# Batch 0's transposed tokens in banks by head pairs; batch 2's first M quarter ahead of one piece of output and its scores behind another

## The chip, the core and the metric

The kernel runs on one core of a Trainium2 chip. The metric is device time in microseconds (us) of one execution; the kernel before has a median of 202.16 us over three runs (202.1 to 202.26). TensorE is written PE in the profile's rows (its weight loads PEld), VectorE DVE, ScalarE ACT, GpSimd POOL and SyncE SP. SP, ACT and POOL also issue DMA transfers; a q behind an engine's name (SPq, POOLq) marks what its queue does. Each engine works through its own list of instructions strictly in order, and waits at an instruction whose semaphores have not come.

## The reference, cut to what matters

There are 8 batches with 8 heads, 512 tokens and 32 state rows of 64 numbers for each head. Attention runs in both directions between tokens and state rows, the two results are laid side by side as rows of 512 numbers, and a two-layer network is applied to every row:

```python
def _attn_ref(x, state):
    scores = scale * np.matmul(x, state.transpose(0, 1, 3, 2))
    a = softmax(scores)                      # over the 32 state rows, 1e-9 in the divisor
    xread = np.matmul(a, state)
    scores2 = scale * np.matmul(state, x.transpose(0, 1, 3, 2))
    a2 = softmax(scores2)                    # over the 512 tokens
    sread = np.matmul(a2, x)
    return np.concatenate([xread, sread], axis=2)

def _moe_ref(x, w_in, w_out):
    h = x @ w_in                             # 512 -> 2048
    g = np.maximum(0.01 * h, h)
    return g @ w_out                         # 2048 -> 512
```

## The kernel before

**What is computed, and in which form.** For the token rows the kernel never forms `xread`. It multiplies the state by the first weight matrix once per batch, M = state · w_in (2 x 128 rows, 2048 columns), and then h = a · M. M is made in four quarters of 512 columns: `a_m(a, c, tag)` (L364) makes quarter c in PSUM banks of the tag given, and `m_evict` (L384) copies it to SBUF. `ff1(a, hT, j)` (L394) makes 128 columns of h as two products over the probabilities `a.aT` and M, in one bank of tag "ph", and ACT applies the leaky relu on the way to `hT` (L403). For batch 0 `piece(0, h0, i, jq)` (L602) multiplies one quarter jq of h by w_out for a quarter i of the tokens; four such pieces make one output bank, which `y_store` copies out (ACT or DVE) and SP stores. From batch 1 on, class `Batch` does the second layer with 7 products instead of 8 (Strassen), in units of two products (`f.unit`, L679), on two banks of tag "py".

**Banks.** Tags "ph" and "py" have two banks each and are handed round in turn; "big" and "sc" are one tile of two banks each. A new user of a bank waits until the last copy out of it has ended. Pieces (0, 0) and (0, 1) hold "py" banks, pieces (0, 2) and (0, 3) the two halves of "big"; batch 1's second layer takes the "py" banks over, bank 1 from piece (0, 0), bank 2 from piece (0, 1).

**The scores chain of a batch.** `a_scores` (L212) makes the scores in "sc" from the transposed tokens `a.xT` and the transposed state. On DVE `a_shift` follows (row maxima L226, spread L234, subtraction L239), `a_max2` (L288, L290), and after an exponential on ACT (L246) `a_probs` (sum L251, L255, reciprocal L258, spread L263, product L264) gives `a.aT`. `a_exp2` on ACT (L296) reads "sc" too and is its last reader. From batch 1 on, xT comes by a DMA transpose that SP issues (L200) once POOL and ACT have cast the batch's tokens; batches 2 and 3 take their state from `st_t[0]`, a DMA transpose issued by SP (L187) behind a cast on POOL (L186).

**The order of the work.** It is written out by hand: the program sets the order on each engine (`manual_schedule`), and nothing is moved by a planner. The parts that matter here:

- The head, 0 to about 10 us. Batch 0's tokens come as four transfers of two heads each (`xf`), and are cast to bf16 by DVE, ACT and POOL (L120). PE transposes them (`x0_half`, L781), for each half u of the tokens into two banks, one for each quarter of the tokens, all four head pairs k in each; `xt0_evict` (L789) copies each bank out, one on DVE and one on ACT. Scores (L796, L811) and maxima (L831) follow.
- POOL issues the loads of w_in (L126), of w_out (L134), of batch 1's tokens (L900) and of batch 2's (L107), in that order; the last load is the last quarter of w_out, which pieces of quarter jq = 3 need.
- From L1000 on PE runs batch 0's sixteen pieces of the second layer, and between them makes batch 1's scores and M and batch 2's first M quarter; from L1063 it adds batch 1's `ff1`.

Of the kernel before, what the change touches and what calls it, by code (L numbers as in the profile page):

```python
# [9 lines left out]
P = 128  # L10
# [6 lines left out]
NK = H // 2  # L17
# [5 lines left out]
BF16 = mybir.dt.bfloat16  # L23
# [7 lines left out]
def kernel(  # L31
# [9 lines left out]
    nc = tc.nc  # L41
# [9 lines left out]
    psum = ctx.enter_context(tc.tile_pool(name="psum", bufs=2, space=bass.MemoryType.PSUM))  # L51
# [5 lines left out]
    VEC, SCA, POO = nc.vector.tensor_copy, nc.scalar.copy, nc.gpsimd.tensor_copy  # L57
# [20 lines left out]
    ident = consts.tile([P, P], BF16, name="ident")  # L78
# [33 lines left out]
    def cast_x(b, h0, h1, copy):  # L112
        copy(  # L113
            xs[b][:, :, h0:h1].rearrange("p t h d -> p h t d"),
            xl[b][:, h0:h1].rearrange("p h (t d) -> p h t d", t=NT),
        )

    def cast_x0(k, t0, t1, copy):
        h = 2 * (k % 2)
        copy(  # L120
            xs[0][:, t0:t1, 2 * k:2 * k + 2].rearrange("p t h d -> p h t d"),
            xf[k // 2][:, h:h + 2, D * t0:D * t1].rearrange("p h (t d) -> p h t d", t=t1 - t0),
        )
# [61 lines left out]
    def state_t(i):  # L185
        POO(stb[i][:], stf[i][:])  # L186
        nc.sync.dma_start_transpose(st_t[i][:], stb[i][:].rearrange("p b q -> p (b q)"))  # L187
# [17 lines left out]
    def st_of(a, g, k):  # L205
        rows = slice(D * g, D * (g + 1))
        if a.b == 0:
            return stbd[rows, k, g ^ (k // 2), :]
        t = st1 if a.b == 1 else st_t[0][:, a.b - 2] if a.b < 4 else st_t[1][:, a.b - 4]
        return t[rows, NS * k:NS * (k + 1)]  # L210

    def a_scores(a):  # L212
        sc = psum.tile([P, 2, S], FP32, name="sc", tag="sc", bufs=1)
        for k in range(NK):
            for g in range(2):
                nc.tensor.matmul(  # L216
                    sc[NS * k:NS * (k + 1), g, :],
                    lhsT=st_of(a, g, k),
                    rhs=a.xT[D * g:D * (g + 1), :, k, :],
                    start=True, stop=True,  # L220
                )
        a.sc = sc
# [141 lines left out]
    def a_m(a, c, tag):  # L364
        if a.M is None:
            a.M = mpool.tile([P, 2, DFF], BF16, name="M", tag="M")
        if tag in ("ph", "py", "phpy"):
            pm = [psum.tile([P, DM], FP32, name="pm", tag=t) for t in (tag[:2], tag[-2:])]
            at = [t[:] for t in pm]
        else:  # L370
            pm = psum.tile([P, 2, DM], FP32, name="pm", tag=tag, bufs=1)
            at = [pm[:, g, :] for g in range(2)]
        for k in range(NK):
            for g in range(2):
                v, r = (k // 2, 2 * (k % 2) + (g ^ (k // 2))) if a.b == 0 else (g, k)
                nc.tensor.matmul(  # L376
                    at[v][NS * r:NS * (r + 1)],
                    lhsT=st_of(a, g, k),
                    rhs=w_in_bf[D * g:D * (g + 1), k, DM * c:DM * (c + 1)],
                    start=True, stop=True,  # L380
                )
        return pm

    def m_evict(a, c, pm, copy):  # L384
        cols = slice(DM * c, DM * (c + 1))
        if isinstance(pm, list):
            for g in range(2):
                copy(a.M[:, g, cols], pm[g][:])
        else:
            copy(a.M[:, :, cols], pm[:])  # L390
# [211 lines left out]
    def piece(b, hT, i, jq, bank=None, copy=SCA, part=range(4)):  # L602
        if jq == 0:
            y = ys[b, i] = Y()
            y.py = psum.tile([P, DM], FP32, name="py", tag="py")[:] if bank is None else bank
        y = ys[b, i]
        for j in (4 * jq + v for v in part):
            nc.tensor.matmul(  # L608
                y.py, lhsT=hT[:, j, P * i:P * (i + 1)], rhs=w_out_bf[:, j, :],
                start=(j == 0), stop=(j == 15),  # L610
            )
        if jq == 3 and copy is not None:
            y_store(b, i, copy)

    def y_store(b, i, copy):
        tag, bufs = (f"yo{i - 2}", 1) if (b, i) in ((0, 2), (0, 3)) else ("ysb", 3)
        ysb = ypool.tile([P, DM], FP32, name="ysb", tag=tag, bufs=bufs)
        copy(ysb[:], ys[b, i].py)
        if b == B:
            for bb in range(4):  # L620
                r0 = (4 * i + bb) * SROW + S
                nc.sync.dma_start(out[r0:r0 + NS, :], ysb[NS * bb:NS * (bb + 1), :])
        else:
            nc.sync.dma_start(rows_of(b)[i], ysb[:])
# [143 lines left out]
    a0, a1, a2 = att_of[:3]  # L768
# [5 lines left out]
    state01()  # L774
    spin(3, "py")

    def x0_half(u):
        pxt = [psum.tile([P, NK, P], BF16, name="pxth", tag=("ph", "py")[u]) for _ in range(2)]
        for k in range(NK):
            for v in range(2):  # L780
                nc.tensor.transpose(  # L781
                    pxt[v][:, k, :],
                    a0.xb[:, 2 * u + v, 2 * k:2 * k + 2, :].rearrange("p h d -> p (h d)"), ident[:],
                )
        return pxt

    def xt0_evict(u, pxt, copies):
        for v, copy in enumerate(copies):
            copy(a0.xT[:, 2 * u + v], pxt[v][:])  # L789

    sct = {}

    def scores0(u, v):
        sct[u, v] = psum.tile([P, NK, 2, NS], FP32, name="sct", tag=("big", "sc")[v], bufs=1)
        for k in range(NK):
            nc.tensor.matmul(  # L796
                sct[u, v][:, k].rearrange("p w n -> p (w n)"),
                lhsT=a0.xT[:, 2 * u + v, k, :],
                rhs=stbd[:, k].rearrange("p g n -> p (g n)"),
                start=True, stop=True,  # L800
            )
# [5 lines left out]
    def rows0(u):  # L807
        scn[u] = psum.tile([P, 2, HT], FP32, name="scn", tag="ph")
        for q in range(2):
            for c in range(NK):  # L810
                nc.tensor.matmul(  # L811
                    scn[u][NS * c:NS * (c + 1), q, :], lhsT=stbd[:, 2 * q + c // 2, c % 2, :],
                    rhs=a0.xT[:, 2 * u:2 * u + 2, 2 * q + c // 2, :], start=(q == 0), stop=False,
                )
# [13 lines left out]
    def max0(u, v):  # L828
        if v == 0:
            m0[u] = att.tile([P, NG], FP32, name="m0", tag="m0")  # L830
        nc.vector.tensor_reduce(  # L831
            out=m0[u][:, H * v:H * (v + 1)],
            in_=sct[u, v][:].rearrange("p k w n -> p (k w) n"), axis=AX.X, op=ALU.max, negate=True,
        )
# [27 lines left out]
    def recip0(u):  # L862
        q = att.tile([P, NG], BF16, name="q0", tag="q0")
        with nc.allow_low_precision(reason="one rounding, of the finished reciprocal"):
            nc.vector.reciprocal(q[:], r0[u][:])
        return q
# [12 lines left out]
    cast_x0(0, 0, NT, VEC)  # L879
    for k in (1, 2):  # L880
        cast_x0(k, 0, 2, VEC)
    cast_x0(3, 0, 2, SCA)
    for k in (1, 2):
        cast_x0(k, 2, NT, VEC)
    cast_x0(3, 2, NT, POO)
    pxt = [x0_half(u) for u in range(2)]
    xt0_evict(0, pxt[0], (VEC, SCA))
    xt0_evict(1, pxt[1], (SCA, VEC))
    x1 = [consts.tile([P, NK, 2 * P], FP32, name="x1", tag=f"x1{u}") for u in range(2)]
    a0.aT = att.tile([P, 2, S], BF16, name="aT", tag="aT")  # L890
    open_xb(1)
# [12 lines left out]
        load_w_out(c, 3 - c)  # L904
    load_x(2, nc.gpsimd)
    load_w_out(3)
    for u in range(2):
        rows0(u)
    for v in range(2):
        scores0(1, v)  # L910
        max0(1, v)
    spread0(scn[0], m, False)
    exp0(0)
    for u in range(2):
# [1 line left out]
    pm = a_m(a0, 0, "big")  # L916
# [3 lines left out]
    q = recip0(0)  # L920
# [7 lines left out]
    q = recip0(1)  # L928
    pm = a_m(a0, 1, "big")
# [3 lines left out]
    h0 = hpool.tile([P, 16, S], BF16, name="hT", tag="hT")  # L933
# [42 lines left out]
    for u, j, tag in (  # L976
# [7 lines left out]
        if (u, j) == (0, 8):  # L984
            pm = a_m(a0, 3, "big")
# [15 lines left out]
    for u in range(2):  # L1001
        piece(0, h0, 1 + u, 0, bank=wide[:, 0] if u else None)
        ps = psum.tile([P, NT, 2, P], BF16, name="pxt2", tag="ph")
        for t in range(NT):
            for v in range(2):
                h = NK * u + 2 * v
# [16 lines left out]
    weights_sum(2, 0, 4, nc.gpsimd)  # L1023
    weights_sum(1, 0, 4, nc.gpsimd)
    state_t(0)
    cast_x(2, 0, 4, SCA)
    for h in range(NK, H):
        cast_x(2, h, h + 1, POO)
    a_open(a2, 2)
    a_xt_dma(a2)  # L1030
    for i in (2, 3):
        piece(0, h0, i, 1)
    m_evict(a1, 3, a_m(a1, 3, "ph"), SCA)
    for g in range(2):
        a_exp2(a1, g)
    load_x(3, nc.sync)
# [1 line left out]
    a_probs(a1)  # L1038
    for i in range(NT):
        piece(0, h0, i, 2)  # L1040
    piece(0, h0, 2, 3, copy=None)
    for n in (2, 1):
        weights_sum(n, 4, 8)
# [15 lines left out]
    def evict(*js):  # L1059
        for j in js:  # L1060
            relu.pop(j)()

    pm = a_m(a2, 0, "sc")  # L1063
    ff(0)
    evict(0)
    ff(1)
    evict(1)
    m_evict(a2, 0, pm, VEC)
    piece(0, h0, 3, 3, copy=None)
    for i in (2, 3):  # L1070
        y_store(0, i, VEC)
# [1 line left out]
    evict(2)  # L1073
    ff(3)
    evict(3)
    a_scores(a2)
    a_shift(a2)
    a_max2(a2)
    piece(0, h0, 0, 3)
    ff(4, 5)  # L1080
    load_state(1, range(0, 2))
    evict(4, 5)
# [23 lines left out]
    pm = [a_m(a2, 1, "big"), a_m(a2, 2, "sc")]  # L1106
# [8 lines left out]
    for b in range(2, B):  # L1115
# [16 lines left out]
        for s in range(16):  # L1132
            fast = nxt is None and 4 <= s < 12
            if fast:
                n = 1 if s in (7, 11) else 2
                k = PACE[s]
# [126 lines left out]
    u, v = [psum.tile([P, 1, HC], FP32, name="yu", tag="ph")[:] for _ in range(2)]  # L1263
# [65 lines left out]
```

## Time and profile before

| what | value |
|---|---|
| median of the runs | 202.16 us |
| profiled execution | 202.11 us, span 200.3 us |
| PE busy | 193.2 us (96%) |
| DVE busy | 160.4 us (80%) |
| ACT busy | 143.5 us (72%) |
| POOL busy | 54.7 us (27%) |
| mean granted clock of PE | 0.999 |

The span is the time from the first to the last instruction of the profiled execution; 1.8 us of its time lie outside. A row of the timeline reads: start, duration, engine, line of the kernel, operation, what it writes and reads, shapes, count; in brackets stands how long the engine had been idle before and what ended that wait. Rows that follow closely on each other are merged, with the count behind an x. Some matmul records can be missing, so a count may be one too low, and matmuls overlap: eight in a row of 512 columns start 0.216 us apart.

### The profile page before, as it was taken

The numbers are of one execution on the slowest core, as the hardware profiler recorded it, in microseconds if no ns is written. First come the engines' busy times: TensorE is split into PE (matmuls) and PEld (weight loads), VectorE is DVE, ScalarE is ACT, GpSimd is POOL, SyncE is SP. The second block draws the span as 40 slices with busy tenths as digits, with TensorE's granted clock in tenths as the row PEclk, the third lists the DMA queues.
The fourth block names the chain that finished last, engine by engine and source line by source line (L and its number), as shares of the span: only waits on it lengthen the run. The fifth ranks groups of instructions, "written<-read, shape, count | busy, mean of one in ns | idle before, by whom it ended". The sixth has DMA issues, their size and how long they took to land.

```text
span 200.3 us, 4974 instructions
## 1 busy us (share of the span) xinstructions
PE 193.2 (96%) x2044; PEld 134.3 (67%) x2066; DVE 160.4 (80%) x248; ACT 143.5 (72%) x264; POOL 54.7 (27%) x81
## 2 busy tenths in 40 slices
PE   7899999999999999999999999999999999999993
PEld 2566633346676767766776677666767788799882
DVE  2666689999999989975997499779978977995622
ACT  3378747599877867978697859787878768767710
POOL 8393074690037004200420040100020024005250
PEclk9999999999999999999999999999999999999999
DMA  5999997999571993359424844290025102310035
GB/s 182 225 207 258 245 293 139 229 286 202 118 216 26 276 272 76 64 206 254 97 41 173 261 73 76 105 164 0 0 108 157 29 0 88 125 56 0 0 95 170
DMA packets 39494, 28.01 MB, mean 140 GB/s; under 512 B 25328, under 2 KB 36720, under 8 KB 39472
## 3 DMA queue, kind: packets, MB, share of 16 engines
q1 hardware_dynamic: 33712, 20.35, 39.4%
q0 software_dynamic: 4928, 6.55, 16.0%
q10 hardware_dynamic: 832, 0.79, 1.3%
q8 instruction: 16, 0.26, 0.6%
q14 instruction: 6, 0.05, 0.1%
HBM read 17.30 MB, written 8.91 MB: 131 GB/s over the span
## 4 chain that ended last, share of the span: by engine, by line
PE 81%; DMA 15%; issue 1%; DVE 1%; ACTq 0%; ACT 0%; POOL 0%
PE yq L679 44%; PE ph L397 20%; DMA w_out_bf<-in_moe_w_out_dram 8%; DMA w_in_bf<-in_moe_w_in_dram 4%; PE pf L475 3%; PE pm L376 3%; PE yu L679 3%; DMA xf<-in_x_dram 2%; PE pl L564 2%; PE psn L342 1%; PE sc L216 1%; PE pyw L608 1%; PE py L608 1%; PE phw L410 1%; PE yz L679 0%
## 5 line engine op out<-in xcount | busy, mean ns | idle before, releaser
L403 ACT ACTIVATE hT<-ph 128x512 bf16<-128x512 f32 x100 | 58.5, 605 | 17.7 <-PE ph L397 11.9
L679 PEld LDWEIGHTS <-su 128*128 128x128 bf16 x480 | 46.0, 98 | 14.8 <-DVE su L668 0.8
L397 PE MATMUL ph<-aT,M 128*128 128x512 bf16 x180 | 54.4, 379 | 0.3
L679 PEld LDWEIGHTS <-hT 128*128 128x128 bf16 x336 | 32.3, 98 | 14.3 <-issue 2.5
L679 PE MATMUL yq<-tw_xf,su 128*128 128x256 bf16 x224 | 31.5, 273 | 0.3
L679 PE MATMUL yq<-w_out_bf,hT 128*128 128x256 bf16 x224 | 31.0, 273 | 0.1
L113 POOL CAST xb<-xl 128x512 bf16<-128x512 f32 (+1 forms) x24 | 13.8, 620 | 47.9 <-DMA xl<-in_x_dram 47.9
L668 DVE TENSOR_TENSOR su<-hT 128x1024 bf16<-128x1024 bf16 (+1 forms) x27 | 19.1, 711 | 6.7 <-ACT hT L403 6.7
L397 PEld LDWEIGHTS <-M 128*128 128x128 bf16 x200 | 19.5, 98 | 5.7 <-issue 0.2
L751 POOL TENSOR_TENSOR yo<-sv,sv 128x512 f32<-128x512 f32 x7 | 9.1, 1295 | 41.6 <-issue 21.3
L688 ACT COPY sv<-yq 128x512 f32<-128x512 f32 x28 | 16.3, 586 | 3.0 <-PE yq L679 2.5
L679 PE MATMUL yq<-w_out_bf,su 128*128 128x256 bf16 x112 | 15.3, 273 | 0.3
L679 PE MATMUL yq<-tw_x,su 128*128 128x256 bf16 x112 | 15.5, 272 | 0.0
L691 DVE TENSOR_TENSOR yo<-yq,sv 128x512 f32<-128x512 f32 x20 | 13.6, 681 | 1.5 <-PE yq L679 1.5
L679 PE MATMUL yq<-tw_x,hT 128*128 128x256 bf16 x104 | 14.5, 273 | 0.0
L390 ACT CAST M<-pm 128x1024 bf16<-128x1024 f32 x12 | 12.2, 1018 | 0.2 <-PE pm L376 0.2
L296 ACT ACTIVATE e<-sc,mcols 128x512 bf16<-128x512 f32 x16 | 11.0, 696 | 0.4 <-DVE mcols L290 0.4
L608 PEld LDWEIGHTS <-hT 128*128 128x128 bf16 x64 | 5.9, 98 | 7.3 <-issue 1.5
L668 DVE TENSOR_TENSOR su<-su,hT 128x1024 bf16<-128x1024 bf16 x14 | 9.7, 692 | 0.5
L288 DVE TENSOR_REDUCE mcol<-sc 128x2 f32<-128x1024 f32 x8 | 9.7, 1216 | 0.0
L226 DVE TRANSPOSE_TENSOR_REDUCE mrow<-sc 128x32 f32<-128x1024 f32 x7 | 8.7, 1242 | 0.5 <-PE sc L216 0.5
L234 DVE STREAM_TRANSPOSE mrowb<-mrow 128x1024 f32<-128x1024 f32 x7 | 8.7, 1245 | 0.2
(174 smaller groups left out, 301.6 us busy)
## 6 DMA issues: line engine op xcount, KB each, us to landing
out_dram<-yo SPq DMA_DIRECT2D x12, 512.0 KB, 2.7
xl<-in_x_dram SPq DMA_DIRECT2D x5, 1024.0 KB, 6.6
w_in_bf<-in_moe_w_in_dram POOLq DMA_DIRECT2D x4, 512.0 KB, 8.1
w_out_bf<-in_moe_w_out_dram POOLq DMA_DIRECT2D x3, 512.0 KB, 15.4
x<-in_x_dram POOLq DMA_DIRECT2D x2, 512.0 KB, 11.5
xl<-in_x_dram POOLq DMA_DIRECT2D x1, 1024.0 KB, 16.6
out_dram<-ysb SPq DMA_DIRECT2D x4, 256.0 KB, 5.6
out_dram<-yo SPq DMA_DIRECT2D x3, 256.0 KB, 2.5
```

The lines of the kernel that those rows point to most:

```text
L113: copy(xs[b][:, :, h0:h1].rearrange("p t h d -> p h t d"), xl[b][:, h0:h1].rearrange("p h (t d) -> p h t d", t=NT),)
L288: nc.vector.tensor_reduce(out=m2[:], in_=a.sc[:], axis=AX.X, op=ALU.max, negate=True)
L296: nc.scalar.activation(out=a.e2[:, g], in_=a.sc[:, g, :], func=AF.Exp, bias=a.m2s[:, g:g + 1], scale=SCALE, accum_out=a.r2[:, g:g + 1],)
L390: copy(a.M[:, :, cols], pm[:])
L397: nc.tensor.matmul(ph[:], lhsT=a.M[:, g, P * j:P * (j + 1)], rhs=a.aT[:, g, :], start=(g == 0), stop=(g == 1),)
L403: nc.scalar.activation(out=hT[:, j, :], in_=ph[:], func=AF.Prelu, alpha=0.01)
L608: nc.tensor.matmul(y.py, lhsT=hT[:, j, P * i:P * (i + 1)], rhs=w_out_bf[:, j, :], start=(j == 0), stop=(j == 15),)
L668: (eng or nc.vector).tensor_tensor(out=S[n][:, ms], in0=u[:, ms], in1=v[:, ms], op=op)
L679: nc.tensor.matmul(bank[:, i, :], lhsT=lhs[:, m, P * i:P * (i + 1)], rhs=rhs[:, m, :], start=(first and m == 0 and (i == 0 or of is not No ...
L688: copy(t[:], bank)
L691: nc.vector.tensor_tensor(out=dst, in0=bank, in1=self.sv[n][:], op=ALU.add)
L751: nc.gpsimd.tensor_tensor(out=self.yo(1)[:, :, HC:], in0=f.sv[7][:], in1=f.sv[5][:], op=ALU.add)
```

## The change

Three places are edited.

1. **The head.** The two banks of each token half are no longer split by token quarter but by head pairs: the first holds pairs 0 to 2 of both quarters, the second holds pair 3. The transposes are put in another order (pairs 0 to 2 of both halves first), the cast of pair 3's first two token quarters goes from ACT to DVE, and for each half ACT copies the larger bank (768 columns) out, DVE the smaller one (256 columns). The second half's scores are interleaved with the row products.
2. **Batch 2's cast and batch 1's last M quarter.** On ACT the copy of batch 1's fourth M quarter now comes ahead of the cast of batch 2's tokens. PE's order there stays as it was.
3. **Batch 2's first M quarter and scores.** The quarter is made in two "ph" banks rather than in "sc", ahead of piece (0, 2) of jq = 3 rather than behind it, and ACT copies it out instead of DVE. Batch 2's scores come behind piece (0, 0) of jq = 3 rather than ahead of it.

```diff
-    def x0_half(u):
-        pxt = [psum.tile([P, NK, P], BF16, name="pxth", tag=("ph", "py")[u]) for _ in range(2)]
-        for k in range(NK):
-            for v in range(2):
-                nc.tensor.transpose(
-                    pxt[v][:, k, :],
-                    a0.xb[:, 2 * u + v, 2 * k:2 * k + 2, :].rearrange("p h d -> p (h d)"), ident[:],
-                )
-        return pxt
-
-    def xt0_evict(u, pxt, copies):
-        for v, copy in enumerate(copies):
-            copy(a0.xT[:, 2 * u + v], pxt[v][:])
+    pxt = {}
+
+    def x0_t(u, k):
+        b = k // 3
+        if (u, b) not in pxt:
+            pxt[u, b] = psum.tile([P, 3 - 2 * b, 2, P], BF16, name="pxth", tag=("ph", "py")[u])
+        for v in range(2):
+            nc.tensor.transpose(
+                pxt[u, b][:, k % 3, v, :],
+                a0.xb[:, 2 * u + v, 2 * k:2 * k + 2, :].rearrange("p h d -> p (h d)"), ident[:],
+            )
+
+    def xt0_evict(u, b, copy):
+        copy(
+            a0.xT[:, 2 * u:2 * u + 2, 3 * b:3 + b].rearrange("p v k q -> p k v q"), pxt[u, b][:]
+        )
...
-    cast_x0(3, 0, 2, SCA)
     for k in (1, 2):
         cast_x0(k, 2, NT, VEC)
+    cast_x0(3, 0, 2, VEC)
     cast_x0(3, 2, NT, POO)
-    pxt = [x0_half(u) for u in range(2)]
-    xt0_evict(0, pxt[0], (VEC, SCA))
-    xt0_evict(1, pxt[1], (SCA, VEC))
+    for u, k in ((0, 0), (1, 0), (0, 1), (0, 2), (1, 1), (1, 2), (0, 3), (1, 3)):
+        x0_t(u, k)
+    for u in range(2):
+        xt0_evict(u, 0, SCA)
+        xt0_evict(u, 1, VEC)
...
-    for u in range(2):
-        rows0(u)
-    for v in range(2):
-        scores0(1, v)
-        max0(1, v)
+    rows0(0)
+    scores0(1, 0)
+    max0(1, 0)
+    rows0(1)
+    scores0(1, 1)
+    max0(1, 1)
...
     state_t(0)
+    for i in (2, 3):
+        piece(0, h0, i, 1)
+    m_evict(a1, 3, a_m(a1, 3, "ph"), SCA)
     cast_x(2, 0, 4, SCA)
     for h in range(NK, H):
         cast_x(2, h, h + 1, POO)
     a_open(a2, 2)
     a_xt_dma(a2)
-    for i in (2, 3):
-        piece(0, h0, i, 1)
-    m_evict(a1, 3, a_m(a1, 3, "ph"), SCA)
...
     for i in range(NT):
         piece(0, h0, i, 2)
+    m_evict(a2, 0, a_m(a2, 0, "ph"), SCA)
     piece(0, h0, 2, 3, copy=None)
...
-    pm = a_m(a2, 0, "sc")
     ff(0)
     evict(0)
     ff(1)
     evict(1)
-    m_evict(a2, 0, pm, VEC)
     piece(0, h0, 3, 3, copy=None)
...
     evict(3)
+    piece(0, h0, 0, 3)
     a_scores(a2)
     a_shift(a2)
     a_max2(a2)
-    piece(0, h0, 0, 3)
     ff(4, 5)
```

## The prediction

> **What bounds the kernel now.** First the page, for the engines and the chain that ended last; then that chain in order of time.
>
> ```profile
> PE 193.2 (96%) x2044; PEld 134.3 (67%) x2066; DVE 160.4 (80%) x248; ACT 143.5 (72%) x264; POOL 54.7 (27%) x81
> PE 81%; DMA 15%; issue 1%; DVE 1%; ACTq 0%; ACT 0%; POOL 0%
> ...
> 9.44 8.21 DMA w_in_bf<-in_moe_w_in_dram
> 17.93 16.57 DMA w_out_bf<-in_moe_w_out_dram
> 34.54 1.02 PE pyw L608 x4
> ```
>
> PE is busy 96% of the span, and from 34.54 us on the chain is PE nearly alone. Ahead of that it runs over the weight loads: the last quarter of w_out is issued at 17.93 and lands at 34.50, and a piece of output starts on it at 34.54. So there are two stages. Up to 34.5 us the transfers set the time, and what PE saves there it spends waiting at the end. After that each wait that PE gains is added to the total. Two rows of the view by windows, and two waits for loads from the timeline, bear this out:
>
> ```profile
> 6.00:18.00 12.00, 11.12 (x225) 7.50 (x226) 8.37 (x20) 8.24 (x16) 6.75 (x11) 1.00 1.24 204
> 39.10:61.20 22.10, 21.80 (x198) 13.77 (x201) 21.50 (x30) 18.82 (x33) 8.99 (x10) 1.00 0.82 200
> ...
> 17.93 0.75 POOL L134 DMA_DIRECT2D w_out_bf<-in_moe_w_out_dram  x1 [1.46 <-DMA w_in_bf<-in_moe_w_in_dram]
> 23.53 0.69 DVE L992 CAST xb<-x 128x1024 bf16<-128x1024 f32 x1 [0.73 <-DMA x<-in_x_dram]
> ```
>
> The second last column is the transfers' share of the 16 DMA engines: 1.24 over 6 to 18 us, none to spare. The last w_out load is not issued before an earlier load has landed (1.46 us of wait), and batch 1's tokens also wait for their transfer. In the second window DVE (third pair of numbers) works 21.50 of 22.10 us: what reaches DVE late there stays late.
>
> **The head.** Its rows in the timeline:
>
> ```profile
> 6.66 0.41 ACT L120 CAST xb<-xf 128x256 bf16<-128x256 f32 x1 [1.25 <-DMA xf<-in_x_dram]
> 7.12 0.73 PE L781 MATMUL pxth<-ident,xb 128*128 128x128 bf16 x10 [0.48 <-ACT xb L120]
> 7.44 1.07 ACT L789 COPY xT<-pxth 128x512 bf16<-128x512 bf16 x2 [0.38 <-PE pxth L781]
> 7.87 0.50 PE L796 MATMUL sct<-stbd,xT 128*128 128x64 bf16 x8
> ```
>
> PE stands 0.48 us for the last head pair, and ten transposes follow. In the new order only pair 3's four follow. Its cast takes about 0.3 us on DVE against 0.41 on ACT, and both halves' first three pairs are ready by 7.0, so ACT can copy from about 6.7. Between the 0.59 us of one of its 512-column copies here and pure scaling (0.88) I take 0.8 for 768 columns, hence 7.5 for the first half; DVE's smaller copy ends near 7.6. The first scores move from 7.87 to about 7.6, and all behind them by 0.25 to 0.3 us. On the path this is worth nothing: at 24 us the cast of batch 1's tokens already holds about a third of it back, and the rest is waited away at 34.5, since a transfer at full load does not land earlier for being issued earlier. For the same reason a head that came out 0.5 us later would cost nothing either.
>
> **The M quarter.** Around 34.5 us, from the timeline, with three rows of the DMA views on landings (the last for the time from 30 to 34 us):
>
> ```profile
> 30.81 1.90 PE L608 MATMUL py<-w_out_bf,hT 128*128 128x512 bf16 x8
> 31.08 1.26 SPq L187 DMA_TRANSPOSE st_t<-stb  x1
> st_t<-stb SPq DMA_TRANSPOSE x1, 3.8
> DMA to landing us min/median/max: 2.4/3.1/3.8
> xT<-xb SPq DMA_TRANSPOSE x1, 4.3
> 35.32 0.22 ACT L296 ACTIVATION_READ_ACCUMULATOR e<-sc,mcols 128x1 f32 x1
> 35.59 0.41 PE L376 MATMUL pm<-w_in_bf,st_t 64*32 64x512 bf16 x8
> 35.93 1.04 PE L397 MATMUL ph<-aT,M 128*128 128x512 bf16 x3
> 36.57 0.60 ACT L403 ACTIVATE hT<-ph 128x512 bf16<-128x512 f32 x1 [1.03 <-PE pm L376]
> ```
>
> Before: sixteen products from 30.81, 0.216 us each, end at 34.27. PE waits for w_out until 34.54 (0.27 lost), runs a piece (0.86), waits 0.09 for ACT to leave "sc" (35.32 + 0.22), makes the quarter at 35.59 and starts `ff1` at 35.93. After: the quarter stands first, and it needs the transposed state. That transpose was issued at 31.08 and landed 3.8 us later, at 34.88. The nearest rows are 2.4 us (the kernel's other transpose of states, the minimum of the range shown) and 4.3 us (the transpose of batch 2's tokens, which SP issues next), so it lands between 33.5 and 35.4. I take 34.88: the edits move neither its issue, which follows POOL's cast, nor the w_out load that shares the engines with it and lands at 34.50. So PE, there at 34.1, stands until 34.92; the quarter takes 0.34 (35.93 - 35.59), the piece, whose weights have come, 0.86, and `ff1` starts at 36.13: **0.20 us later**. The wait for "sc" is gone, and the one for the state is longer than both old ones. What stands behind PE's new wait is the piece, whose weights have come by then, and all of batch 1's `ff1`.
>
> The Trainium skill, in "DMA: Bandwidth & Descriptors", section "Anatomy of one DMA", gives a transfer (there one issued by GpSimd) a fixed 2.0 us and the rest by its bytes. By that this transpose of 64 KB would land near 33.2 (an estimate from that page), PE would not wait, and the time would be that of rival 1; the row of 3.8 us does not agree. The same page, in "Queues, rings and completion order", says that a completion on one DMA engine comes only after all earlier writes of that engine, those of other queues too; the landing 0.38 us behind w_out's agrees with that.
>
> ACT's two copies of the quarter lie in its 1.03 us of idle time. The earlier copy of batch 1's last quarter fits ahead of batch 2's cast, which waits for its tokens anyhow:
>
> ```profile
> 28.30 0.41 PE L376 MATMUL pm<-w_in_bf,st 64*32 64x512 bf16 x8
> 28.77 1.07 ACT L388 CAST M<-pm 128x512 bf16<-128x512 f32 x2 [1.10 <-PE pm L376]
> 32.17 1.04 ACT L113 CAST xb<-xl 128x1024 bf16<-128x1024 f32 x1 [0.90 <-DMA xl<-in_x_dram]
> ```
>
> Copies start 0.47 us behind their products (28.30 to 28.77 for an earlier quarter), so 35.39 to 36.46 here. The two "ph" banks come free at 35.9 and 36.5, just ahead of the `ff1` that want them at 36.13 and 36.56. If a bank came free later, PE would stand for the difference; I take none. DVE is relieved of a copy of 1.2 us (the size of that at 49.08 below), but cannot use the time: its next long work waits for batch 2's scores.
>
> **Batch 2's scores.** They start DVE's long chain (timeline of DVE and PE):
>
> ```profile
> 38.62 0.41 PE L216 MATMUL sc<-xT,st_t 64*32 64x512 bf16 x8
> 39.10 1.25 DVE L226 TRANSPOSE_TENSOR_REDUCE mrow<-sc 128x32 f32<-128x1024 f32 x1
> 44.18 0.68 DVE L618 COPY ysb<-py 128x512 f32<-128x512 f32 x1
> 45.02 1.04 PE L679 MATMUL yq<-w_out_bf,hT 128*128 128x256 bf16 x8
> 47.92 0.69 DVE L264 TENSOR_TENSOR aT<-e,qb 128x1024 bf16<-128x1024 bf16 x1
> 48.73 0.17 DVE L304 RECIPROCAL qall<-r 128x2 f32<-128x2 f32 x1
> 49.08 1.23 DVE L390 CAST M<-pm 128x1024 bf16<-128x1024 f32 x1 [0.18 <-PE pm L376]
> 49.38 0.59 PE L397 MATMUL ph<-aT,M 128*128 128x512 bf16 x2
> ```
>
> From 36.13, four `ff1` (1.73), two pieces (1.73) and PE's 0.10 of changeover give 39.69, against 38.62: the chain starts **1.07 us later**, and DVE cannot catch up. (Piece (0, 0) itself ends no later than before: its copy on ACT and its store keep their places on ACT and SP, and cost nothing.) What hid the chain, place by place:
> - The copy of piece (0, 1) sits in that chain and ends at 44.86, now 45.93. Batch 1's second layer wants that "py" bank with the fifth of the eight products from 45.02 (0.109 apart), at 45.46, now 45.66. PE stands 0.31: **0.51 in all**.
> - `aT` ends at 48.61, now 49.68; PE wants it at 49.38 + 0.51. No wait.
> - DVE's copy of the next quarter had waited 0.18 for PE; that is used up: 49.97 for 49.08. DVE stays 0.88 late.
>
> ```profile
> 60.19 0.45 DVE L290 TENSOR_SCALAR mcols<-mcol 128x2 f32<-128x2 f32 x1
> 60.67 0.69 ACT L296 ACTIVATE e<-sc,mcols 128x512 bf16<-128x512 f32 x1 [0.39 <-DVE mcols L290]
> 61.82 0.61 ACT L403 ACTIVATE hT<-ph 128x512 bf16<-128x512 f32 x1
> 62.79 0.59 PE L397 MATMUL ph<-aT,M 128*128 128x512 bf16 x2
> ```
>
> - In batch 3's chain ACT already waits for DVE at 60.67; 0.88 later, the relu at 61.82 frees its bank at 63.31 instead of 62.43, and the `ff1` at 62.79 + 0.51 wants it. PE stands another 0.06. Past that, the lateness dies in waits of DVE.
>
> Sum: 0 (head) + 0.20 + 0.31 + 0.06 = **0.57 us**. The profiled execution took 202.11 us, the median 202.16; I forecast **202.7**.
>
> **The rivals.** Less than 0.2% (0.4 us, 201.76 to 202.56) is about what a measurement of this kernel cannot tell from no change.
>
> 1. Not slower: the state has landed when PE comes. If its transpose needs 2.4 us rather than 3.8, the quarter fills the wait for w_out, the piece starts at 34.54 and `ff1` at 35.41, 0.52 earlier. The scores are still 0.35 late on DVE, and the bank waits leave -0.14: 202.0. The sum is zero for a landing near 34.3. For it speaks the one short row, against it the 3.8 us of this very transpose, whose neighbours on the engines stay the same. 17%. The fixed cost that the Trainium skill states in "DMA: Bandwidth & Descriptors" ("Anatomy of one DMA") would give this outcome.
> 2. Nobody waits for DVE's lateness, if those banks come free otherwise; then 0.20 alone: 202.3. Against it stands the order of DVE's rows. 13%.
> 3. More waits. SP's transpose of batch 3's tokens stands behind the store of the late copy:
>
> ```profile
> 45.39 2.69 SPq L200 DMA_TRANSPOSE xT<-xb  x1
> xT<-xb SPq DMA_TRANSPOSE x1, 5.9
> 51.87 0.41 PE L216 MATMUL sc<-xT,st_t 64*32 64x512 bf16 x8
> ```
>
>    Moved by 1.07 it lands at 52.36, when PE wants it (51.87 + 0.51). With 0.3 us more, or the state landing at 35.2, the time is 203.0. 14%.
> 4. Faster: the head's 0.3 us also brings the loads forward, because POOL issues w_in's last quarter behind the head's maxima (9.44). With rival 1 that makes -0.4: 201.7. Against it: 1.24 at 6 to 18 us. 12%.
>
> The forecast has 44%. Faster: rival 4, 12%. Same: rivals 1 and 2 and a little of the forecast, 32%. Slower: the rest, 56%. The range takes in rivals 1, 2 and 3 with the late landing: 201.9 to 203.2; the forecast's own is 202.5 to 202.9.
>
> **What the profile after would show.** The head's scores near 7.6 and w_out's landing still at 34.5; the quarter (L376) first and waiting for the DMA of `st_t` until 34.9; `ff1` at 36.1; the row maxima at 40.2; a wait of DVE's copy near 45.7. The forecast is wrong if the quarter starts near 34.1, if w_out lands earlier, or if the products near 45.7 do not wait.

## The result and the profile after

The changed kernel takes 202.70 us (median of 6 runs, 202.55 to 203.07); the kernel before, on the same chip, took 202.06 us (6 runs, 201.76 to 202.26). The ratio is 1.0035, with a 95% interval from 1.0022 to 1.0048: slower, by about 0.7 us. The forecast was 202.7 us, slower. The profiled execution of the changed kernel took 202.76 us with a span of 201.0, against 202.11 and 200.3 before.

On the page of the changed kernel, the busy times and the chain that ended last:

```profile
PE 193.6 (96%) x2044; PEld 134.0 (67%) x2066; DVE 159.6 (79%) x248; ACT 144.8 (72%) x265; POOL 54.2 (27%) x81
PE 70%; DVE 11%; DMA 11%; POOL 3%; issue 2%; ACT 1%; SPq 0%; POOLq 0%
```

PE's work is nearly what it was. The chain is what changed: VectorE (DVE) had 1% of it and now has 11%. In order of time (start, length, engine or transfer, tile, line) the chain of the changed kernel shows where it leaves PE and where it comes back:

```profile
31.01 3.70 DMA st_t<-stb
...
40.01 1.26 DVE mrow L226
41.29 1.26 DVE mrowb L234
42.57 1.23 DVE sh L239
43.80 1.14 DVE mcol L288
44.96 0.25 DVE mcols L290
45.21 0.59 DVE ysb L618
...
60.03 1.14 DVE mcol L288
61.20 0.46 DVE mcols L290
61.67 0.78 ACT e L296 x2
...
62.93 0.51 ACT hT L403
...
63.48 0.59 PE ph L397 x2
```

The part shown starts with the landing of the transposed state (31.01 + 3.70 = 34.71), goes through batch 2's scores on DVE from 40.01 on, stays on DVE for twenty microseconds, passes through ACT's exponential and relu (`hT`, done at 63.44), and returns to PE for good at 63.48.

The three waits that PE gained, from the timeline of the changed kernel (the bracket is the idle time just before the group, and what ended it):

```profile
34.75 0.41 PE L376 MATMUL pm<-w_in_bf,st_t 64*32 64x512 bf16 x8 [0.58 <-DMA st_t<-stb]
35.97 1.03 PE L397 MATMUL ph<-aT,M 128*128 128x512 bf16 x4
39.52 0.41 PE L216 MATMUL sc<-xT,st_t 64*32 64x512 bf16 x8
45.85 0.60 PE L679 MATMUL yq<-w_out_bf,hT 128*128 128x256 bf16 x4 [0.20 <-DVE ysb L618]
63.48 0.59 PE L397 MATMUL ph<-aT,M 128*128 128x512 bf16 x2
```

Against the same instructions of the kernel before, `ff1` starts 0.04 us later (35.97 for 35.93), the product that wants the "py" bank 0.40 later (45.85 for 45.45), and the `ff1` at 63.48 is 0.69 later (62.79 before). The span is longer by the same 0.7, so nothing more is lost behind 63.48, and nothing is won back. Part by part: 0.04 + 0.36 + 0.29. (The row at 63.48 has no bracket; its first product starts 0.40 us behind the one before it, where 0.11 is usual.)

### The profile page after: what moved, and what is told of

It reads as the page before. It is cut to its first block, busy times and chain, and to the rows that moved or that the text cites. A ratio compares the mean times of both kernels' runs of the same rounds, so it can differ in the third digit from the quotient of the medians.

```text
span 201.0 us, 4975 instructions
## 1 busy us (share of the span) xinstructions
PE 193.6 (96%) x2044; PEld 134.0 (67%) x2066; DVE 159.6 (79%) x248; ACT 144.8 (72%) x265; POOL 54.2 (27%) x81
## 4 chain that ended last, share of the span: by engine, by line
PE 70%; DVE 11%; DMA 11%; POOL 3%; issue 2%; ACT 1%; SPq 0%; POOLq 0%
PE yq L679 38%; PE ph L397 16%; DMA w_out_bf<-in_moe_w_out_dram 7%; PE pf L475 3%; PE yu L679 3%; PE pm L376 3%; DMA xf<-in_x_dram 2%; DVE su L668 2%; DMA st_t<-stb 2%; PE pl L564 2%; DVE mrowb L234 1%; DVE mrow L226 1%; DVE sh L239 1%; DVE mcol L288 1%; POOL tw_x L645 1%
## 5 line engine op out<-in xcount | busy, mean ns | idle before, releaser
L668 DVE TENSOR_TENSOR su<-hT,su 128x2048 bf16<-128x2048 bf16 (+1 forms) x8 | 9.4, 1175 | 0.0
```

Source lines behind the costliest of these rows:

```text
L668: (eng or nc.vector).tensor_tensor(out=S[n][:, ms], in0=u[:, ms], in1=v[:, ms], op=op)
```

## The experiments

**First four runs: the parts apart.** The head alone; all but the head; the M quarter alone (with the head); the late scores alone (with the head).

Head alone: the kernel before, with the head of the changed one.

```diff
...
-    pxt = [x0_half(u) for u in range(2)]
-    xt0_evict(0, pxt[0], (VEC, SCA))
-    xt0_evict(1, pxt[1], (SCA, VEC))
+    for u, k in ((0, 0), (1, 0), (0, 1), (0, 2), (1, 1), (1, 2), (0, 3), (1, 3)):
+        x0_t(u, k)
+    for u in range(2):
+        xt0_evict(u, 0, SCA)
+        xt0_evict(u, 1, VEC)
...
```

> The kernel before with the change's head alone. Theory (the transfers set the time up to 34.5 us): the first scores near 7.4 us as in the changed kernel, PE some 0.2 us early until it waits for the last w_out load, a wait of about 0.5 us there instead of 0.27, and a total within 0.15 us of the kernel before. Rival (the earlier issue brings the loads forward): w_out lands 0.15 to 0.3 us earlier and the total is 0.15 to 0.3 us less.

Measured: 202.18 us, ratio 1.0007 (0.9998 to 1.0016). No change that can be told. Its chain has w_out's last load landing at 34.62 (17.73 + 16.89), no earlier than in the kernel before:

```profile
9.22 8.22 DMA w_in_bf<-in_moe_w_in_dram
17.73 16.89 DMA w_out_bf<-in_moe_w_out_dram
...
34.66 1.02 PE L608 MATMUL pyw<-w_out_bf,hT 128*128 128x512 bf16 x4 [0.30 <-DMA w_out_bf<-in_moe_w_out_dram]
```

The load was issued 0.20 us earlier and landed 0.12 later, so the rival falls. What the head wins is waited away here: from the end of the product before, reckoned at 0.216 us each, PE waits 0.46 us for the load, against 0.27 in the kernel before.

All but the head: the changed kernel, with the old head.

```diff
...
-    for u, k in ((0, 0), (1, 0), (0, 1), (0, 2), (1, 1), (1, 2), (0, 3), (1, 3)):
-        x0_t(u, k)
-    for u in range(2):
-        xt0_evict(u, 0, SCA)
-        xt0_evict(u, 1, VEC)
+    pxt = [x0_half(u) for u in range(2)]
+    xt0_evict(0, pxt[0], (VEC, SCA))
+    xt0_evict(1, pxt[1], (SCA, VEC))
...
```

> The changed kernel with the head of the kernel before. Theory: the whole loss is in the other two edits, so the total is 0.5 to 0.8 us above the kernel before, as with the head. If the head brings the loads forward: some 0.2 us slower still than the changed kernel.

Measured: 203.08 us, ratio 1.0052 (1.0036 to 1.0068). That is 0.97 us above the kernel before (202.11 in that round), more than the theory's 0.5 to 0.8, and nearer to the rival. Its interval overlaps that of the changed kernel, so that the head saves something there isn't shown; and w_out landed no later than in the changed kernel (34.37 against 34.33). In its profiled execution PE waits longer for the copy of piece (0, 1) than in the changed kernel (0.53 us in the bracket against 0.20), because the small DVE instruction ahead of that copy took 0.58 us instead of 0.25, beside a cast of POOL that had started at 44.98:

```profile
45.03 0.58 DVE L290 TENSOR_SCALAR mcols<-mcol 128x2 f32<-128x2 f32 x1
...
46.25 0.60 PE L679 MATMUL yq<-w_out_bf,hT 128*128 128x256 bf16 x4 [0.53 <-DVE ysb L618]
```

The M quarter alone: the changed kernel, with batch 2's scores back ahead of piece (0, 0).

```diff
-    piece(0, h0, 0, 3)
     a_scores(a2)
     a_shift(a2)
     a_max2(a2)
+    piece(0, h0, 0, 3)
```

> The changed kernel with batch 2's scores back ahead of piece (0, 0). Theory: the early M quarter itself costs only what its wait for the transposed state costs, and the rest of the loss came by the scores: batch 1's first ff1 starts within 0.2 us of 35.93, the waits of PE for DVE's copy near 45.8 us and for ACT's relu near 63.5 us are gone, and the total is 0 to 0.25 us above the kernel before. Rival (the early quarter is what costs): 0.4 us or more above.

Measured: 202.32 us, ratio 1.0015 (1.0006 to 1.0025). PE waits for the state and for nothing of DVE's later on:

```profile
35.06 0.41 PE L376 MATMUL pm<-w_in_bf,st_t 64*32 64x512 bf16 x8 [0.74 <-DMA st_t<-stb]
36.28 1.03 PE L397 MATMUL ph<-aT,M 128*128 128x512 bf16 x4
```

The late scores alone: the kernel before with the new head, and piece (0, 0) ahead of batch 2's scores.

```diff
+    piece(0, h0, 0, 3)
     a_scores(a2)
     a_shift(a2)
     a_max2(a2)
-    piece(0, h0, 0, 3)
```

> The kernel before with the change's head and batch 2's scores behind piece (0, 0); the M quarter stays where it was. Theory: the first ff1 starts near 35.8 us, the scores 0.87 us (one piece) later than with the head alone, and DVE's lateness comes back as waits of PE near 45.8 and 63.5 us: 0.3 to 0.7 us above the kernel before. Rival (the quarter is what costs): within 0.15 us of it.

Measured: 202.66 us, ratio 1.0025 (1.0010 to 1.0041). Of the two waits that were expected, only the first came. The eight products on the "py" banks take 1.31 us instead of 1.04 (the fifth waits 0.28), and at 63.43 the `ff1` follows without a wait:

```profile
45.37 1.31 PE L679 MATMUL yq<-w_out_bf,hT 128*128 128x256 bf16 x8
```

The landing of w_out differs between these executions by more than the effects that are looked for. Reckoned from it, the profiled executions can be compared. All columns are microseconds of the trace; "rest" is the end of the span less w_out's landing.

| kernel | w_out lands | st_t lands | `ff1` starts | span | rest |
|---|---|---|---|---|---|
| before | 34.50 | 34.88 | 35.93 | 200.29 | 165.79 |
| head alone | 34.62 | 35.01 | 36.04 | 200.41 | 165.79 |
| quarter (and head) | 34.64 | 35.02 | 36.28 | 200.67 | 166.03 |
| late scores (and head) | 34.84 | 35.25 | 36.28 | 200.94 | 166.10 |
| changed kernel | 34.33 | 34.71 | 35.97 | 200.99 | 166.66 |
| all but the head | 34.37 | 34.78 | 36.04 | 201.47 | 167.09 |

In these single executions the head is worth nothing, the quarter ahead of its piece costs 0.24, the late scores 0.31, and both together 0.87, not 0.55: the third wait, at 63.48, is in neither execution of one part alone. The runs don't bear out that the parts add up to less than the whole: by their ratios the quarter costs about 0.3 us, the late scores 0.5, both 0.7, with intervals wider than the difference. The last experiment says why the third wait can be there or not with the same late scores.

**Is DVE's lateness paid once or at each meeting?** The changed kernel, with DVE's copy of piece (0, 1) moved ahead of batch 2's `a_max2`; the other engines keep their order.

```diff
     a_shift(a2)
-    a_max2(a2)
     ff(4, 5)
...
     piece(0, h0, 1, 3, copy=VEC)
+    a_max2(a2)
     a_exp(a2)
```

> The changed kernel; in VectorE's program alone the copy of piece (0,1) now stands ahead of the two instructions of batch 2's a_max2 (mcol 1.22 us and mcols, some 0.2 to 0.6 us). TensorE, ScalarE, GpSimd and SyncE keep their order. Theory (one late VectorE chain, which TensorE meets at two places, of which the later one decides): the copy ends about 1.4 us sooner, and TensorE's wait of 0.20 us at 45.85 is gone, but a_max2 now ends later and aT no sooner, so the wait at batch 2's later steps is as long as before; TensorE is late by as much at 64 us, and the total stays within 0.2 us of the changed kernel: 202.5 to 202.8 us. Rival (the two waits add up, as the prediction's sum has it): what the wait at 45.85 cost (0.36 us more than before) is won back, the total is 202.2 to 202.4 us.

Measured: 202.74 us, ratio 1.0025 (1.0011 to 1.0040). PE's wait near 45.8 is gone, and comes back at 62.49 (0.25 us, for an operand sum of DVE) and 63.68 (0.31, as in the changed kernel):

```profile
43.88 0.68 DVE L618 COPY ysb<-py 128x512 f32<-128x512 f32 x1
44.48 1.21 DVE L288 TENSOR_REDUCE mcol<-sc 128x2 f32<-128x1024 f32 x1
...
62.49 1.05 PE L679 MATMUL yq<-w_out_bf,su 128*128 128x256 bf16 x8
63.68 0.59 PE L397 MATMUL ph<-aT,M 128*128 128x512 bf16 x2
```

From w_out's landing to the end it is 166.69 against 166.66: in the profiled executions nothing was won. (The two intervals overlap widely.) Here the wait taken away ahead of the last one only let PE arrive earlier at the next.

**Does an earlier issue bring the state earlier?** The changed kernel, with the states' cast and transpose ahead of the second of GpSimd's weight sums.

```diff
     weights_sum(2, 0, 4, nc.gpsimd)
-    weights_sum(1, 0, 4, nc.gpsimd)
     state_t(0)
+    weights_sum(1, 0, 4, nc.gpsimd)
```

> The changed kernel, with the cast and the transpose of the states st_t moved ahead of the second of GpSimd's two weight sums: the cast is at about 28.5 instead of 30.6 us, SyncE issues the transpose at about 29.0 instead of 31.0. Theory (a transfer by transpose completes only behind the load of w_out that was issued ahead of it): st_t still lands 0.3 to 0.5 us behind w_out's last load, at about 34.6 to 35.0; TensorE waits for it as long as now, and the total is that of the changed kernel within 0.2 us, 202.5 to 202.9. Rival (a fixed time from the issue, 3.7 us as now): it lands at about 32.7, TensorE does the M quarter in its wait for w_out, and the total falls by 0.2 to 0.4 us, to 202.3 to 202.5.

Measured: 203.05 us, ratio 1.0046 (1.0027 to 1.0066): no gain. The issue moved from 31.01 to 29.46, and the transfer took 5.80 us instead of 3.70. PE's row and the chain's:

```profile
29.46 5.80 DMA st_t<-stb
...
35.31 0.41 PE L376 MATMUL pm<-w_in_bf,st_t 64*32 64x512 bf16 x8 [0.80 <-DMA st_t<-stb]
```

It landed at 35.26, and w_out's last load in that execution at 35.06. The state stayed behind w_out, as the theory has it, but by 0.21 us rather than 0.3 to 0.5, and the time lies above the ranges of both theory and rival (though its interval overlaps that of the changed kernel); why is open. The same early issue with the scores at their old place:

```diff
     weights_sum(2, 0, 4, nc.gpsimd)
-    weights_sum(1, 0, 4, nc.gpsimd)
     state_t(0)
+    weights_sum(1, 0, 4, nc.gpsimd)
...
-    piece(0, h0, 0, 3)
     a_scores(a2)
     a_shift(a2)
     a_max2(a2)
+    piece(0, h0, 0, 3)
```

> The changed kernel with batch 2's scores back at their old place ahead of piece (0,0), and with the states cast and sent early, as in the run before this one. If st_t stays behind w_out's last load: TensorE waits for st_t some 0.9 us at 34 to 35, ff(0) starts some 0.24 us later than in the kernel before (reckoned from w_out's landing), and the total is 202.2 to 202.5 us. If st_t lands at about 32.7: the quarter lies in TensorE's wait for w_out, no wait is added, ff(0) starts 0.2 to 0.4 us earlier than in the kernel before, and the total is 201.7 to 201.9 us, under the kernel before.

Measured: 202.48 us, ratio 1.0014 (1.0002 to 1.0026), as for the quarter alone. Issued at 29.27, the state took 5.6 us and landed at 34.85, 0.30 behind w_out's 34.55 (views of the transfers; the last two columns are KB and us from issue to landing):

```profile
w_out_bf<-in_moe_w_out_dram POOLq DMA_DIRECT2D x1, 512.0 KB, 17.1
st_t<-stb SPq DMA_TRANSPOSE x1, 5.6
```

So with an issue up to 1.8 us earlier, which is still behind that of w_out's last load, the quarter doesn't fill the gap that PE has there. Next, something that doesn't wait for the state.

**Filling PE's wait for w_out.** The kernel before, with w_out's last load as two loads of half the size.

```diff
-    load_w_out(3)
+    load_w_out(3, 2)
```

> The kernel before, in which w_out's last load (its rows j 12 to 15, issued by GpSimd) is made as two of half the size; nothing else is changed. Theory (w_out's last landing sets the time of everything behind 34 us, and st_t comes behind it): the first half lands about 1 us ahead of the second, TensorE does two of the four matmuls of piece (0,2) (0.43 us) in the wait that it now has for the load; ff(0) starts 0.2 to 0.45 us sooner relative to the last landing, and the total is 201.7 to 202.0 us, if no wait for st_t takes its place. Rival (the load is only the first of several things that come at the same time): TensorE waits for st_t, or for batch 1's aT, by as much, and the total is that of the kernel before within 0.1 us. A third: one more descriptor program on GpSimd delays the loads, and the total is 0.1 to 0.3 us over the kernel before.

Measured: 202.01 us, ratio 0.9990 (0.9979 to 1.0000). The halves landed at 33.37 and 34.72, and PE's wait for w_out shrank from 0.27 to 0.12 us; but at the M quarter it then waited 0.45 us, against 0.09 before, for the second exponential of ScalarE (ACT), which frees the "sc" bank. (Both without the 0.09 us that PE takes there to change over, at the earlier quarters as well.) That is the rival in which something else comes at the same time, though not one of the two things that it named. Next, the first two products of piece (0, 3) between the halves of piece (0, 2):

```diff
-    load_w_out(3)
+    load_w_out(3, 2)
...
-    piece(0, h0, 2, 3, copy=None)
+    piece(0, h0, 2, 3, copy=None, part=(0, 1))
+    piece(0, h0, 3, 3, copy=None, part=(0, 1))
+    piece(0, h0, 2, 3, copy=None, part=(2, 3))
...
-    piece(0, h0, 3, 3, copy=None)
+    piece(0, h0, 3, 3, copy=None, part=(2, 3))
```

> As the run before this one, and the first two matmuls of piece (0,3), of the same quarter of w_out, are put between the halves of piece (0,2). Theory: where TensorE still waits for the second half of the load, this hides up to 0.43 us more of it; ff(0) starts 0.0 to 0.2 us sooner than with the split alone if a wait for the second half was left there, or up to 0.43 us later with the piece at (0,3)'s place shorter by as much, so that nothing is lost further on; total 201.6 to 202.0 us. Rival: as before, st_t or aT is late by then, total within 0.1 us of the kernel before.

Measured: 201.75 us, ratio 0.9974 (0.9965 to 0.9983): faster than the kernel before, and so than the changed one. The timeline shows PE with work up to the M quarter, where it stands 0.22 us, 0.09 of them the changeover and 0.13 the wait for ACT:

```profile
32.56 3.19 PE L608 MATMUL pyw<-w_out_bf,hT 128*128 128x512 bf16 x14
34.96 0.70 ACT L296 ACTIVATE e<-sc,mcols 128x512 bf16<-128x512 f32 x1
35.53 0.22 ACT L296 ACTIVATION_READ_ACCUMULATOR e<-sc,mcols 128x1 f32 x1
35.80 0.41 PE L376 MATMUL pm<-w_in_bf,st_t 64*32 64x512 bf16 x8
36.14 0.82 PE L397 MATMUL ph<-aT,M 128*128 128x512 bf16 x3
```

`ff1` still starts at 36.14, but 0.43 us of the next piece is done by then. The last step puts batch 1's first `ff1` into those 0.22 us, ahead of the quarter:

```diff
-    pm = a_m(a2, 0, "sc")
     ff(0)
     evict(0)
+    pm = a_m(a2, 0, "sc")
     ff(1)
```

> The kernel of the run before this one (w_out's last load in two, the first two matmuls of piece (0,3) between the halves of piece (0,2)), in which batch 1's ff(0) now stands ahead of batch 2's M quarter on TensorE. There TensorE waited 0.22 us for ScalarE's second exponential, which frees the scores' bank at 35.75, ahead of the M quarter at 35.80; batch 1's aT was done at 35.28 and ff(0) needs neither the bank nor st_t. Theory (what is won at 35 us goes through to the end): ff(0) starts at about 35.6, the M quarter at about 36.0 without a wait, and what follows is 0.2 us sooner: 201.5 us, against 201.75. Rival: VectorE copies the quarter 0.2 us later than now, and its chain of batch 2's scores, or ScalarE's relu of ff(0), gives it back: 201.7 to 201.9 us.

Measured: 201.72 us, ratio 0.9978 (0.9969 to 0.9987), not to be told from the run before it. The first `ff1` had to wait for batch 1's `aT`, ready at 35.37, and started at 35.57; the quarter then began at 36.09, later than in the run before (35.80), and piece (0, 3) 0.14 us earlier. The 0.2 us weren't there to be won: the changeover stays, and PE's wait for ACT became one for `aT`.

**What made the third wait?** The prediction had 0.06 us at 62.8, the trace 0.29. DVE reached batch 3's `mcols` 1.0 us late instead of 0.88. The rows of DVE and GpSimd (POOL) in the changed kernel:

```profile
58.31 1.17 POOL L113 CAST xb<-xl 128x512 bf16<-128x512 f32 x2 [13.13 <-DMA xl<-in_x_dram]
59.01 1.02 DVE L668 TENSOR_TENSOR su<-hT,su 128x1024 bf16<-128x1024 bf16 x1
59.95 1.21 DVE L288 TENSOR_REDUCE mcol<-sc 128x2 f32<-128x1024 f32 x1
61.20 0.44 DVE L290 TENSOR_SCALAR mcols<-mcol 128x2 f32<-128x2 f32 x1
```

and in the kernel before:

```profile
58.35 0.68 DVE L668 TENSOR_TENSOR su<-hT,su 128x1024 bf16<-128x1024 bf16 x1
58.48 1.02 POOL L113 CAST xb<-xl 128x512 bf16<-128x512 f32 x1 [13.11 <-DMA xl<-in_x_dram]
```

The same sum takes 0.68 us where it starts ahead of POOL's cast, which then takes 1.02; and 1.02 where a cast (0.6 each) has just begun. Whoever comes second waits. DVE came second, being 0.66 us late, and POOL 0.17 us early.

What the sum pays is the rest of the cast under way. In the changed kernel it starts at 59.01 and the next cast at 59.43: 0.42 us left, and the sum takes 0.34 longer. The run with the state's early issue has the same orders on DVE and PE and is as late, but there the sum starts just ahead of a cast's end:

```profile
59.01 0.62 POOL L113 CAST xb<-xl 128x512 bf16<-128x512 f32 x1 [13.67 <-DMA xl<-in_x_dram]
59.48 0.69 DVE L668 TENSOR_TENSOR su<-hT,su 128x1024 bf16<-128x1024 bf16 x1
```

The next cast starts at 59.57, 0.09 us behind the sum, which takes 0.69; PE's `ff1` at 63.66 doesn't wait, and the rest of that execution behind w_out's landing is 166.08 us instead of 166.66 (0.17 of this because the state landed nearer to w_out). The run with the late scores alone is alike: 0.08 us left, 0.68, no wait. All but the head, and the run with DVE's copy first, have 0.45 and 0.54 us left, sums of 1.04 and 1.13, and the wait (0.31 in both). So the third wait hangs on where in POOL's row of casts the late sum falls; how often that happens in the timed executions isn't known. To see whether another order avoids that cost, `a_max2`, which reads PSUM, goes ahead of that sum in the changed kernel:

```diff
-                    before.f.sums(3, 0, 4)
                     a_max2(nxt)
+                    before.f.sums(3, 0, 4)
                     before.f.sums(3, 4, 8)
```

> The changed kernel; of VectorE's program in batch 2's loop alone, batch 3's a_max2 (mcol, which reads PSUM, and mcols) now stands ahead of the first half of the third operand sum (su<-hT,su). In the changed kernel that su took 1.02 us at 59.01 (0.68 in the kernel before): it began to do work when GpSimd's cast, under way since 58.87, ended at 59.43, and mcols, ScalarE's exponential and the relu that TensorE waits for at 63.48 (0.29 us) came later by as much. Theory (that collision made the last 0.29 us of the loss): mcol starts at 59.0, mcols ends about 0.6 to 1.0 us sooner, TensorE's wait at 63.48 is gone, and the total is 202.4 us (202.3 to 202.5). Rival (VectorE is late by then whatever its order): the wait comes back at the products that use su, at about 62 to 62.5, and the total stays at 202.6 to 202.8.

Measured: 203.17 us, ratio 1.0044 (1.0029 to 1.0059). The theory falls, the rival holds:

```profile
60.84 1.70 DVE L668 TENSOR_TENSOR su<-hT,su 128x1024 bf16<-128x1024 bf16 x2
...
61.57 1.05 PE L679 MATMUL yq<-w_out_bf,su 128*128 128x256 bf16 x8 [0.32 <-DVE su L668]
```

The wait for the relu is gone, and PE waits at 61.57 for the sum that was put back (0.32 us in the bracket). The collision explains the third wait, but this order doesn't take its cost out: at 60 us DVE owes PE two things, and is late with whichever stands second.

## Why the prediction was right, and where it wasn't

The time and the side were right; the sum was 0.57 and the profiled executions differ by 0.70 in span. Two of its terms were clearly off, in opposite directions.

- **The head: worth 0.** Right, for the reason given: with the head alone, the time from w_out's landing to the end is the same 165.79. The size of the step was not: the first scores came at 7.35, 0.5 us earlier, where 7.6 was forecast; ACT's copies of 768 columns took 0.8 us each as assumed, but the first could begin at 6.50, and the second had to follow it. It made no difference. Rival 4 (the head brings the loads forward) falls with the same run.
- **The M quarter: 0.20.** The mechanism was right: the quarter waits for `st_t`, and that wait is longer than the two that it replaces. Against the clock of the span `ff1` moved by 0.04 only, because all transfers of that execution came 0.17 us earlier (w_out 34.33 for 34.50, `st_t` 34.71 for 34.88). From w_out's landing `ff1` moved by 0.21 (1.64 us against 1.43), and with the quarter moved alone the whole cost was 0.24. The step that failed is "34.88" as a time of the clock; as "0.38 behind w_out" it held in both. Rival 1 (the state has landed when PE comes) needed the transfer to last 2.4 us from its issue. The early issue refutes it: the landing stayed behind w_out's, 5.8 us from the issue. The fixed 2.0 us that the Trainium skill gives in "DMA: Bandwidth & Descriptors", section "Anatomy of one DMA", is not what this transfer shows; what the same page says in "Queues, rings and completion order" agrees with it.
- **The scores, 1.07 us later.** They came at 39.52 instead of 38.62, 0.90 later; the missing 0.17 is the transfers' again.
- **The bank of piece (0, 1): 0.31.** Measured: 0.36. Right in place and mechanism; the copy ended at 45.80 on DVE, and the fifth product followed it. Rival 2 (nobody waits for DVE) falls.
- **`aT`, and the M copy.** No wait for `aT`, as said. DVE's lateness at the M copy was 0.68 (49.76 for 49.08), not 0.88, by the same 0.17.
- **The relu at 63 us: 0.06.** Measured: 0.29. This is the term that was mis-sized. The prediction carried DVE's lateness unchanged from 49 to 60 us; the row of `su` grew by 0.34 us in between, since it met POOL's casts the other way round. Had it not, 0.66 of lateness against PE's 0.40 would have left no wait there: the slack of 0.36 (62.43 to 62.79) was larger than the difference. So this wait comes from the collision, and the two executions with the same late scores and no collision, in which PE doesn't wait here, show it. That the prediction had a wait at this place is therefore partly luck: it came by a step that the sum doesn't have. The last run adds only that one other order of DVE's work doesn't save it.
- **Batch 3's tokens (rival 3).** SP issued that transpose at 46.30, it landed at 51.90, and PE did not wait for it.

So the 202.7 is partly luck: 0.16 less at the first term, 0.05 and 0.23 more at the others. What carried the verdict is that both moves put something needed behind something late, and that DVE had no idle time to absorb it.

## What to carry to other kernels

Time a wait for a transfer against the load that is ahead of it on the same engines, not against its own issue: here issuing it 1.6 us earlier moved nothing, while splitting the load ahead of it, and giving PE work on the half that had come, won 0.26%. An engine that is busy through twenty microseconds passes a late start on, and what it meets later can cost more or nothing: where a last wait stood behind it, taking one away in the middle won nothing here. And compare executions from the landing that sets their time, since that alone moved by more here than what was to be measured; but even so one execution isn't the kernel: the same order on DVE and PE was 0.58 us apart in two executions, half of that by a collision.

## What the hardware showed that was not expected

- The transposed state landed 0.21 to 0.41 us behind w_out's last load in all thirteen profiled executions, with issues from 29.27 to 31.69 us, and with w_out landing from 34.33 to 35.06. The Trainium skill's "DMA: Bandwidth & Descriptors" (section "Queues, rings and completion order") says that a completion on one DMA engine waits for all earlier writes of that engine, those of other queues too; that agrees with these landings. Whether it is that order or the state's share of loaded engines, no run here tells apart.
- The order in which DVE and POOL start decides who waits: DVE's sum 0.68 us and POOL's cast 1.02, or the sum 1.02 and the cast ahead of it 0.6. Six executions in which the sum starts during a cast give its price: with 0.08, 0.09, 0.31, 0.42, 0.45 and 0.54 us to the next cast's start the sum takes 0.68, 0.69, 0.92, 1.02, 1.04 and 1.13 us. The Trainium skill's "SBUF — State Buffer", section "SBUF: two separate sides", describes this: both use one pair of ports, the first to start holds it for its whole instruction, and an operation of DVE with two inputs in SBUF needs it, against an operation of POOL that reads SBUF. The rows agree. A shift of a few tenths of a microsecond between two engines was enough to turn a wait around.
- w_out's last load, made as one transfer, took between 16.6 and 17.1 us from its issue. Where nothing else differs behind it, the landing goes through to the end of the span: with the head alone it came 0.12 us later than in the kernel before, and the span was 0.12 longer.
